# Key-value state in eight full steps of four heads, in a Hedgehog attention with a gated MLP

## The chip, the cores and the metric

The kernel runs on one core of one Trainium2 chip. The metric is the time of one execution on the device in microseconds (us). The engines are named as in the profile: PE is TensorE (matmuls; PEld its weight loads), DVE is VectorE, ACT is ScalarE, POOL is GpSimd, and SP issues most of the DMAs.

## The reference

One sequence of S = 2048 tokens with D = 640 features, 32 heads of 20 features, an MLP of F = 1536:

```python
xn = layernorm(x)
q, k, v = split_heads(xn @ wqkv)                       # 32 heads of 20
phi_q = concat([softmax(q @ w_phi), softmax(-q @ w_phi)])   # 40 features a head
phi_k = concat([softmax(k @ w_phi), softmax(-k @ w_phi)])
kv  = sum_s phi_k[s].T @ v[s]                          # 40 x 20 for each head
z   = sum_s phi_k[s]                                   # 40 for each head
o   = (phi_q @ kv) / (phi_q @ z + 1e-6)
s   = merge_heads(o) @ wo
g   = silu(gelu(xn @ w1 + b1) @ w2 + b2)
out = x + s * g
```

All is float32. The large products are computed in three passes of split operands (high x high, high x low, low x high; `PASSES`), each at fp32r.

## The kernel before

**The first part, up to about 249 us in the profile,** walks over 16 tiles of 128 tokens. For each tile t the keys are projected (`project`, L331), turned into features (`feat1`, `feat2`, `key_fin`: maxima, exponentials, sums for each head), and the values are projected into a tile `v` whose 32 heads stand 21 columns apart: 20 values and a column of ones, which makes the normaliser z with the same matmul. After every second tile, `kv_pair` calls `kv_acc` for the last two finished tiles, so there are eight such calls.

**`kv_acc`** adds one tile of tokens to the key-value state, in one PSUM bank `kv`. Every head h is one matmul in full float32 (L402): its 32 columns of `v` are the weights (20 values, the ones, and columns that belong to the next head and are ignored), its 40 columns of features are streamed. The output has 32 partitions, so four heads fit side by side, on partitions 32e to 32e + 31 with e = 0 to 3. A step is one value of s: the heads that write columns 40s to 40s + 39. Heads stand in groups of three, because a block of 120 feature rows (three heads) is what the later steps use; there are eleven such groups, the last with two heads. Group 4g + e stands on the partitions of e, in columns 120g to 120g + 119. So g = 0 and 1 give three steps each of four heads, and g = 2 gives two steps of three heads and one of two: nine steps.

**The state afterwards.** `kv_rest` (L600) adds the last pair and copies the bank into the tile `kvr` (three activations; the parts without a head are set to zero by two memsets of POOL). `kv_norm` (L623), in the first unit of the MLP, brings the row of z of each e to DRAM in the order of the heads (four stores, one more for the last group), and loads it back broadcast to all partitions (`zrep`, `zf`). `kv_state` (L610), in unit 6 of the MLP, transposes `kvr` in three matmuls, and builds from it the block-diagonal weights: `bdk`, ten blocks of 120 rows and 64 columns, each three heads (L616, one masked copy on DVE), and `bdl` for the last two heads (L620, three copies). `num` (L780, L787) multiplies them by the features of the queries, in the last part.

**The second part, from about 249 to 546 us,** is the MLP, in 12 units (two halves of the tokens by six groups of 256 hidden features). A unit has 54 matmuls of the first layer (`part`, L649) and 60 of the second (`down`, L678), 512 columns each. Beside them the queries of the tiles are normalised by z (`q_norm`, L724 the first step of it on POOL) and written transposed to DRAM (`phi_t`). The eight PSUM banks go round: `bankB()` takes the next one, and a bank comes back after eight allocations.

**The third part** is the output projection (`finish`, L833) for four chunks of 512 tokens, the gate and the residual.

The order of instructions is written out by hand: `phase1` for PE and SP, `startup` and `ffn` for all engines. SP issues its DMAs strictly in the order of the code.

**Buffers.** On-chip memory is given out in the order of the pools: `const` (with `bdk`, `bdl`, and at its end `kvr`), then `slabs` (23 buffers of 5120 bytes in each partition), `rows` (11 of 2816), `small`, and behind them `xpool` and later `late`. Some tiles only fill space:

```python
    xpool.tile([P, 16], F32, name="xpad")
    const.tile([P, 8], F32, name="align")
```

Of the kernel before, what the change touches and what calls it, by code (L numbers as in the profile page):

```python
# [8 lines left out]
F32 = mybir.dt.float32  # L9
F32R = mybir.dt.float32r  # L10
AF = mybir.ActivationFunctionType
OP = mybir.AluOpType
AX = mybir.AxisListType

S, D, H, DH, F = 2048, 640, 32, 20, 1536
P = 128
NT = S // P
# [8 lines left out]
NFT = 11  # L26
# [20 lines left out]
def hedgehog_gated_mlp_kernel(ctx: ExitStack, tc: tile.TileContext, x, xt_in, wqk, bd, wv, wo, w1, b1, w2, b2, out_t):  # L47
    nc = tc.nc
    const = ctx.enter_context(tc.tile_pool(name="const", bufs=1))
# [31 lines left out]
    def slab(dt, name, shape=(P, 2, D)):  # L81
        return slabs.tile(list(shape), dt, tag="S", name=name)
# [7 lines left out]
    def bankB(name="pB"):  # L90
        return pools["B"].tile([P, 512], F32, tag="B", name=name)
# [7 lines left out]
    z_dram = dram.tile([1440], F32, name="z_dram")  # L99
    st_dram = dram.tile([NT // 2, 2, P, 2], F32, name="st_dram")  # L100

    ident = const.tile([P, P], F32, name="ident")
# [13 lines left out]
    mask = const.tile([P, 3], F32, name="mask")  # L116
# [17 lines left out]
    bdk = const.tile([P, 10, 64], F32, name="bdk")  # L134
# [251 lines left out]
    kvp = [None]  # L386
# [6 lines left out]

    def kv_acc(t, phi, v):
        ps = kvp[0]
        for g in range(3):
            for r in range(3):
                for e in range(4):
                    h = 3 * (4 * g + e) + r
                    if 4 * g + e < NFT and h < H:  # L400
                        s = 3 * g + r
                        nc.tensor.matmul(ps[32 * e:32 * e + 32, 40 * s:40 * s + 40], v[:, 21 * h:21 * h + 32],  # L402
                                         phi[:, 40 * h:40 * h + 40], start=t == 0 and s == 0, stop=t == NT - 1,
                                         skip_group_check=True)

    vs, es, phis, xns, wk_s, wq_s = {}, {}, {}, {}, [], []

    def kv_pair(t):
        for u in (t, t + 1):
            kv_acc(u, phis.pop(u), vs.pop(u))  # L410
# [55 lines left out]
    one = nc.const_aps.tensor(1.0, [P, P], F32)  # L466
# [126 lines left out]
    t = NT - 1  # L593
# [5 lines left out]

    def kv_rest():  # L600
        kv_pair(NT - 2)
        kvr = const.tile([P, 360], F32, name="kvr")
        nc.gpsimd.memset(kvr[64:96, 320:360], 0.0)
        nc.gpsimd.memset(kvr[96:, 240:360], 0.0)
        for p, a, b in ((P, 0, 240), (96, 240, 320), (64, 320, 360)):
            nc.scalar.activation(kvr[:p, a:b], kvp[0][:p, a:b], AF.Copy)
        return kvr


    def kv_state(kvr):  # L610
        nc.gpsimd.memset(bdk[:, :, 60:], 0.0)
        ps = bankB()
        for g, m in enumerate((P, P, 96)):
            nc.tensor.transpose(ps[:120, g * P:g * P + m], kvr[:m, 120 * g:120 * g + 120], ident[:m, :m])
        s3 = ps[:120, :320].rearrange("p (f r) -> p f r", r=32)
        nc.vector.tensor_tensor(bdk[:120, :, :60].rearrange("p f (h d) -> p f h d", d=20),  # L616
                                s3[:, :, None, :20].to_broadcast([120, 10, 3, 20]),
                                mask[:120, None, :, None].to_broadcast([120, 10, 3, 20]), op=OP.mult)
        for r in range(3):
            nc.vector.tensor_tensor(bdl[:80, 40 * r:40 * r + 40].rearrange("p (h d) -> p h d", d=20),  # L620
                                    ps[:80, None, 320:340].to_broadcast([80, 2, 20]),
                                    mask[:80, :2, None].to_broadcast([80, 2, 20]), op=OP.mult)
    def kv_norm(kvr):  # L623
        zv = z_dram.rearrange("(g e r) -> e g r", e=4, r=120)
        for e, m in enumerate((3, 3, 2, 2)):
            nc.sync.dma_start(zv[e:e + 1, :m], kvr[32 * e + 20:32 * e + 21, :120 * m].rearrange("p (g r) -> p g r", r=120))
        nc.sync.dma_start(z_dram[1200:2 * D].unsqueeze(0), kvr[84:85, 240:320])
        zf = slab(F32, "zrep")[:].rearrange("p a b -> p (a b)")
        nc.sync.dma_start(zf, z_dram[:2 * D].partition_broadcast(P))
        return zf  # L630
# [132 lines left out]
    def load_phi(c, js, home=None):  # L763
        out = {}
        for j in js:
            ph = slab(F32, "phT", (P, 2, CW)) if home is None else home.tile([P, 2, CW], F32, tag="L", name="phT")
            if j < 5:
                nc.sync.dma_start(ph[:120], phi_t[c][240 * j:240 * j + 240, :].rearrange("(e p) t -> p e t", p=120))
            else:
                nc.sync.dma_start(ph[:80, 0], phi_t[c][1200:, :])  # L770
            out[j] = ph
        return out
# [78 lines left out]
    def w2_raw(g):  # L851
        return [load_raw(w2[f * P:(f + 1) * P, :]) for f in range(g * GF, (g + 1) * GF)]

    kvr = kv_rest()
    e_last = feat1(project(next(queries), wq_s))
    startup.close()
# [6 lines left out]
    for unit in range(units):  # L863
        h, g = divmod(unit, NG)
# [13 lines left out]
        else:  # L878
            wo_r = [load_raw(wo[j * P:(j + 1) * P, :]) for j in range(5)]
            phi = load_phi(ORDER[0], range(6))  # L880
# [52 lines left out]
        if unit == 0:  # L933
            zf = kv_norm(kvr)
# [29 lines left out]
        if unit == NG:  # L964
            kv_state(kvr)
# [123 lines left out]
```

## Time and profile before

| | us |
|---|---|
| median of 3 runs | 662.39 |
| lowest, highest | 662.28, 663.07 |
| the profiled execution | 662.16 |
| its span, first to last instruction | 660.5 |

| engine | busy us | share of the span | instructions |
|---|---|---|---|
| PE | 655.2 | 99% | 4447 |
| DVE | 473.0 | 72% | 720 |
| POOL | 381.2 | 58% | 351 |
| ACT | 228.2 | 35% | 321 |

The granted clock of TensorE was 1.000 over the span. The DMAs moved 126.05 MB, 191 GB/s on average. In the rows that follow, a row of the chain has its start and its length in us, the engine, the tile and the line, and xN instructions. A row of an engine's timeline has start, length, engine, line, operation, tiles, shape and count, and in brackets the idle time before it and what ended that.

### The profile page before, as it was taken

The numbers are of one execution on the slowest core, as the hardware profiler recorded it, in microseconds if no ns is written. First come the engines' busy times: TensorE is split into PE (matmuls) and PEld (weight loads), VectorE is DVE, ScalarE is ACT, GpSimd is POOL, SyncE is SP. The second block draws the span as 40 slices with busy tenths as digits, with TensorE's granted clock in tenths as the row PEclk, the third lists the DMA queues.
The fourth block names the chain that finished last, engine by engine and source line by source line (L and its number), as shares of the span: only waits on it lengthen the run. The fifth ranks groups of instructions, "written<-read, shape, count | busy, mean of one in ns | idle before, by whom it ended". The sixth has DMA issues, their size and how long they took to land.

```text
span 660.5 us, 11388 instructions
## 1 busy us (share of the span) xinstructions
PE 655.2 (99%) x4447; PEld 568.5 (86%) x4447; DVE 473.0 (72%) x720; ACT 228.2 (35%) x321; POOL 381.2 (58%) x351
## 2 busy tenths in 40 slices
PE   9999999999999999999999999999999999999997
PEld 8999999999999998888888888888888886776776
DVE  5887665888777556768978968759889899753232
ACT  3523213332332227352452454751232425113220
POOL 3654254849477456857778776364472966343231
PEclk9999999999999999999999999999999999999999
DMA  8920142834272226537899799695769499999942
GB/s 322 340 81 1 6 152 87 250 82 156 42 200 77 95 88 224 175 107 251 235 249 313 182 414 331 95 338 217 157 219 236 93 273 210 311 232 265 282 169 80
DMA packets 157950, 126.05 MB, mean 191 GB/s; under 512 B 88656, under 2 KB 125520, under 8 KB 157000
## 3 DMA queue, kind: packets, MB, share of 16 engines
q1 hardware_dynamic: 155592, 114.84, 60.3%
q10 hardware_dynamic: 2304, 10.49, 4.3%
q8 instruction: 35, 0.57, 0.3%
q14 instruction: 19, 0.16, 0.1%
HBM read 80.20 MB, written 45.10 MB: 190 GB/s over the span
## 4 chain that ended last, share of the span: by engine, by line
PE 93%; DMA 4%; DVE 1%; POOL 1%; issue 0%; SPq 0%; ACT 0%; POOLq 0%
PE pA L331 28%; PE pB L678 25%; PE pB L649 22%; PE pB L833 11%; PE pB L780 3%; PE kv L402 2%; DMA xt<-in_x_dram 2%; DMA raw<-in_wv_dram 1%; DMA folds<-in_wqk_dram 1%; PE pA L172 1%; PE pB L787 1%; POOL wv L147 0%; DMA st_dram<-pst 0%; PE pA L317 0%; POOL e L352 0%
## 5 line engine op out<-in xcount | busy, mean ns | idle before, releaser
L678 PE MATMUL pB<-hs,w2s 128*128 128x512 f32 x720 | 166.0, 390 | 0.0
L678 PEld LDWEIGHTS pB<-hs,w2s 128*128 128x128 f32 x720 | 134.9, 188 | 29.5 <-DVE oT L784 0.8
L649 PE MATMUL pB<-xp,w1s 128*128 128x512 f32 x324 | 81.3, 389 | 0.0
L649 PE MATMUL pB<-xd,w1s 128*128 128x512 f32 x324 | 79.3, 389 | 0.0
L833 PE MATMUL pB<-oT,wo 128*128 128x512 f32 (+2 forms) x315 | 73.3, 384 | 0.0
L357 ACT ACTIVATE e<-e 128x1280 f32<-128x1280 f32 x32 | 40.7, 1273 | 91.9 <-POOL e L352 91.4
L649 PEld LDWEIGHTS pB<-xd,w1s 128*128 128x128 f32 x324 | 60.8, 188 | 12.6
L649 PEld LDWEIGHTS pB<-xp,w1s 128*128 128x128 f32 x324 | 60.8, 188 | 12.6
L833 PEld LDWEIGHTS pB<-oT,wo 128*128 128x128 f32 x315 | 57.6, 188 | 16.0 <-DVE oT L784 1.6
L370 POOL TENSOR_TENSOR eq<-eq,rc 128x1280 f32<-128x1280 f32 x16 | 37.9, 2368 | 55.9 <-DVE rc L737 38.7
L370 POOL TENSOR_TENSOR e<-e,rc 128x1280 f32<-128x1280 f32 x16 | 39.0, 2439 | 47.4 <-DVE rc L390 47.1
L687 DVE TENSOR_TENSOR y<-pB,y 128x512 f32<-128x512 f32 x100 | 63.1, 676 | 1.4 <-PE pB L678 1.4
L352 POOL TENSOR_TENSOR e<-nr,e 128x640 f32<-128x640 f32 x32 | 45.6, 1425 | 29.9 <-DVE nr L351 26.6
L331 PE MATMUL pA<-wv,xp 128*128 128x320 f32 x384 | 60.5, 310 | 0.3 <-POOL wv L147 0.3
L331 PE MATMUL pA<-wk,xp 128*128 128x320 f32 x384 | 59.7, 310 | 0.0
L654 ACT ACTIVATE pB<-pB,b1t 128x512 f32<-128x512 f32 x48 | 31.8, 662 | 78.8 <-DVE pB L916 28.9
L331 PE MATMUL pA<-wq,xp 128*128 128x320 f32 x384 | 58.8, 309 | 0.1
L331 PEld LDWEIGHTS pA<-wv,xp 128*128 128x128 f32 x384 | 57.0, 188 | 0.5 <-POOL wv L147 0.5
L331 PEld LDWEIGHTS pA<-wq,xp 128*128 128x128 f32 x384 | 56.9, 188 | 0.3 <-PE pA L331 0.3
L331 PEld LDWEIGHTS pA<-wk,xp 128*128 128x128 f32 x384 | 56.9, 188 | 0.1
L724 POOL TENSOR_TENSOR ez<-eq,zrep 128x1280 f32<-128x1280 f32 x16 | 47.3, 2958 | 1.4 <-DMA eq<-e_dram 1.4
L430 POOL TENSOR_TENSOR w1s<-raw,w1s 128x640 fp32r<-128x640 f32 (+1 forms) x18 | 27.0, 1498 | 31.9 <-ACT w1s L429 31.9
(138 smaller groups left out, 996.1 us busy)
## 6 DMA issues: line engine op xcount, KB each, us to landing
raw<-in_w_dram SPq DMA_DIRECT2D x42, 320.0 KB, 4.8
e_dram<-e ACTq DMA_DIRECT2D x16, 640.0 KB, 3.5
eq<-e_dram SPq DMA_DIRECT2D x16, 640.0 KB, 5.7
phi_t<-eq SPq DMA_DIRECT2D x64, 160.0 KB, 3.2
phT<-phi_t SPq DMA_DIRECT2D x20, 480.0 KB, 9.7
xt<-in_x_dram SPq DMA_DIRECT2D x16, 320.0 KB, 7.1
xres<-in_xt_dram SPq DMA_DIRECT2D x20, 256.0 KB, 9.2
out_dram<-xres SPq DMA_DIRECT2D x18, 256.0 KB, 5.8
```

Of the source, the lines that this page charges most:

```text
L331: nc.tensor.matmul(ps[:, hf, :HALF], stat_x(q, o, k, a), ws[k][:, b, hf * HALF:(hf + 1) * HALF], start=n == 0, stop=n == 3 * KC - 1)
L352: nc.gpsimd.tensor_tensor(e5[:, :, :, 1, :], nr[:, :, :, None].to_broadcast([P, 2, 16, DH]), e5[:, :, :, 0, :], op=OP.subtract)
L357: nc.scalar.activation(ef, ef, AF.Exp)
L370: nc.gpsimd.tensor_tensor(e3, e3, rc[:, :, None].to_broadcast([P, 64, DH]), op=OP.mult)
L430: nc.gpsimd.tensor_tensor(sl[:, 1, :n], src, sl[:, 0, :n].bitcast(F32), op=OP.subtract)
L649: nc.tensor.matmul(bank[ch][:], tl[:, a, off + wo_:off + wo_ + P], mov(blk, b), start=new and n == 0, stop=n == len(mms) - 1, skip_group_c ...
L654: nc.scalar.activation(ps, ps, AF.Gelu_apprx_tanh, bias=b1t[:, f:f + 1])
L678: nc.tensor.matmul(ps[:], ws[i][:, b, d * P:(d + 1) * P], hs[o][i][:, a, :], start=i == n == 0, stop=(i, n) == (GF - 1, 2), skip_group_che ...
L687: nc.vector.tensor_tensor(y, ps[:], y, op=OP.add)
L724: nc.gpsimd.tensor_tensor(zv, ef, zf, op=OP.mult)
L780: nc.tensor.matmul(po[64 * e:64 * e + 64, :], bdk[:120, 2 * j + e, :], ph[:120, e, :], start=True, stop=True)
L833: nc.tensor.matmul(ps[:, mv], w, o[:, mv], start=n == 0, stop=n == 15, skip_group_check=True)
```

## The change

`kv_acc` gets eight steps of four heads. The first six are as before (groups 0 to 7). The last eight heads, 24 to 31, are spread over the four positions: heads 24 + 2e and 25 + 2e stand on the partitions of e, in columns 240 to 319. The groups of three that the later steps want are put together in `kv_state`: `kvr` has 400 columns, the last 80 a second copy of columns 240 to 319, so that windows of 120 columns can be transposed (four transposes of 128 rows), and DVE takes each head from the block where it lies (five masked copies for `bdk`, three for `bdl`). `kv_norm` stores two pieces for every e, eight stores in all. The two memsets go, since no part of the bank is empty.

```diff
     def kv_acc(t, phi, v):
         ps = kvp[0]
-        for g in range(3):
-            for r in range(3):
-                for e in range(4):
-                    h = 3 * (4 * g + e) + r
-                    if 4 * g + e < NFT and h < H:
-                        s = 3 * g + r
-                        nc.tensor.matmul(ps[32 * e:32 * e + 32, 40 * s:40 * s + 40], v[:, 21 * h:21 * h + 32],
-                                         phi[:, 40 * h:40 * h + 40], start=t == 0 and s == 0, stop=t == NT - 1,
-                                         skip_group_check=True)
+        for s in range(8):
+            for e in range(4):
+                h = 3 * (4 * (s // 3) + e) + s % 3 if s < 6 else 24 + 2 * e + s - 6
+                nc.tensor.matmul(ps[32 * e:32 * e + 32, 40 * s:40 * s + 40], v[:, 21 * h:21 * h + 32],
+                                 phi[:, 40 * h:40 * h + 40], start=t == 0 and s == 0, stop=t == NT - 1,
+                                 skip_group_check=True)
...
     def kv_rest():
         kv_pair(NT - 2)
-        kvr = const.tile([P, 360], F32, name="kvr")
-        nc.gpsimd.memset(kvr[64:96, 320:360], 0.0)
-        nc.gpsimd.memset(kvr[96:, 240:360], 0.0)
-        for p, a, b in ((P, 0, 240), (96, 240, 320), (64, 320, 360)):
-            nc.scalar.activation(kvr[:p, a:b], kvp[0][:p, a:b], AF.Copy)
+        kvr = const.tile([P, 400], F32, name="kvr")
+        nc.scalar.activation(kvr[:, :320], kvp[0][:, :320], AF.Copy)
+        nc.scalar.activation(kvr[:, 320:], kvp[0][:, 240:320], AF.Copy)
         return kvr
 
 
     def kv_state(kvr):
         nc.gpsimd.memset(bdk[:, :, 60:], 0.0)
         ps = bankB()
-        for g, m in enumerate((P, P, 96)):
-            nc.tensor.transpose(ps[:120, g * P:g * P + m], kvr[:m, 120 * g:120 * g + 120], ident[:m, :m])
-        s3 = ps[:120, :320].rearrange("p (f r) -> p f r", r=32)
-        nc.vector.tensor_tensor(bdk[:120, :, :60].rearrange("p f (h d) -> p f h d", d=20),
-                                s3[:, :, None, :20].to_broadcast([120, 10, 3, 20]),
-                                mask[:120, None, :, None].to_broadcast([120, 10, 3, 20]), op=OP.mult)
+        for i, o in enumerate((0, 120, 240, 280)):
+            nc.tensor.transpose(ps[:120, i * P:(i + 1) * P], kvr[:, o:o + 120], ident[:])
+
+        def heads_of(f, n, blk, h, m):
+            src = ps[:120, 32 * blk:32 * (blk + n)].rearrange("p (f r) -> p f r", r=32)
+            nc.vector.tensor_tensor(bdk[:120, f:f + n, 20 * h:20 * (h + m)].rearrange("p f (h d) -> p f h d", d=20),
+                                    src[:, :, None, :20].to_broadcast([120, n, m, 20]),
+                                    mask[:120, None, h:h + m, None].to_broadcast([120, n, m, 20]), op=OP.mult)
+
+        heads_of(0, 8, 0, 0, 3)
+        heads_of(8, 1, 8, 0, 2)
+        heads_of(8, 1, 9, 2, 1)
+        heads_of(9, 1, 13, 0, 1)
+        heads_of(9, 1, 14, 1, 2)
         for r in range(3):
             nc.vector.tensor_tensor(bdl[:80, 40 * r:40 * r + 40].rearrange("p (h d) -> p h d", d=20),
-                                    ps[:80, None, 320:340].to_broadcast([80, 2, 20]),
+                                    ps[:80, None, 352:372].to_broadcast([80, 2, 20]),
                                     mask[:80, :2, None].to_broadcast([80, 2, 20]), op=OP.mult)
+
     def kv_norm(kvr):
-        zv = z_dram.rearrange("(g e r) -> e g r", e=4, r=120)
-        for e, m in enumerate((3, 3, 2, 2)):
-            nc.sync.dma_start(zv[e:e + 1, :m], kvr[32 * e + 20:32 * e + 21, :120 * m].rearrange("p (g r) -> p g r", r=120))
-        nc.sync.dma_start(z_dram[1200:2 * D].unsqueeze(0), kvr[84:85, 240:320])
+        zv = z_dram[:960].rearrange("(g e r) -> e g r", e=4, r=120)
+        zl = z_dram[960:2 * D].rearrange("(e r) -> e r", e=4)
+        for e in range(4):
+            one = kvr[32 * e + 20:32 * e + 21]
+            nc.sync.dma_start(zv[e:e + 1], one[:, :240].rearrange("p (g r) -> p g r", r=120))
+            nc.sync.dma_start(zl[e:e + 1], one[:, 240:320])
         zf = slab(F32, "zrep")[:].rearrange("p a b -> p (a b)")
```

## The prediction

> **What bounds the kernel now.** I read the first page first, for the engine that carries the span and for the chain that ended last.
>
> ```profile
> PE 655.2 (99%) x4447; PEld 568.5 (86%) x4447; DVE 473.0 (72%) x720; ACT 228.2 (35%) x321; POOL 381.2 (58%) x351
> PE 93%; DMA 4%; DVE 1%; POOL 1%; issue 0%; SPq 0%; ACT 0%; POOLq 0%
> PE pA L331 28%; PE pB L678 25%; PE pB L649 22%; PE pB L833 11%; PE pB L780 3%; PE kv L402 2%; DMA xt<-in_x_dram 2%; DMA raw<-in_wv_dram 1%; DMA folds<-in_wqk_dram 1%; PE pA L172 1%; PE pB L787 1%; POOL wv L147 0%; DMA st_dram<-pst 0%; PE pA L317 0%; POOL e L352 0%
> ```
>
> TensorE (PE) is busy for 99% of the span and is 93% of the chain. Next I asked for what TensorE ever waited, and then for the chain in order of time.
>
> ```profile
> PE pA L469 <- PEq L1079: 0.8, 1, 0.8
> PE pA L172 <- DMA folds<-in_wqk_dram: 0.6, 1, 0.6
> PE pA L331 <- POOL wv L147: 0.3, 1, 0.3
> ```
>
> ```profile
> 2.19 4.89 DMA xt<-in_x_dram
> 7.09 7.19 DMA raw<-in_wv_dram
> 14.29 6.81 DMA folds<-in_wqk_dram
> ...
> 27.68 3.49 PE pA L331 x22
> ...
> 47.21 1.42 PE kv L402 x119
> ...
> 243.12 1.42 PE kv L402 x119
> ...
> 261.40 13.60 PE pB L678 x60
> ...
> 421.88 0.30 PE pB L614 x3
> ```
>
> The waits answer has only these three rows for TensorE, 1.7 us in all. Two lie in the start-up, the third ends at 27.68 us. From there to 657 us no row names another engine or a transfer that TensorE waited for, so a nanosecond saved there shortens the run, and one added lengthens it, until some other engine becomes late. The key-value accumulation, L402, stands on that chain as eight bursts of 1.42 us, one for each pair of token tiles (the first at 47.21, the last at 243.12). The wide matmuls around it (L331, L678, L649, L833) are 86% of the chain.
>
> **Part 1, the accumulation: eight steps instead of nine.** No instruction is removed: a token tile still has 32 matmuls, one for each head, and the order of all engines outside the lines of the diff is unchanged in the compiled program. What changes is how they stand in the four column positions of the array. Before, a tile has six steps of four heads, two of three and one of two; after, eight of four. Whether that saves time depends on what a step costs. The answer for line L402 and the number of its records begun by a given moment of the first burst show it (columns: stretch, its length, busy time of PE and records in it, clock, DMA share, GB/s):
>
> ```profile
> L402 PEld LDWEIGHTS kv<-e,v x1024: 105/112/118, 47.1 to 244.3; 128*32 128x32 f32 x171
> L402 PE MATMUL kv<-e,v x1024: 202/202/224, 47.1 to 244.3; 128*32 128x40 f32 x171
> ...
> 47.10:47.38 0.28, 0.23 (x24) 1.00 0.00 0
> 47.10:47.45 0.35, 0.30 (x32) 1.00 0.00 0
> ...
> 47.10:47.59 0.49, 0.45 (x48) 1.00 0.00 0
> 47.10:47.66 0.56, 0.52 (x54) 1.00 0.00 0
> 47.10:47.73 0.64, 0.59 (x60) 1.00 0.00 0
> 47.10:47.77 0.67, 0.63 (x64) 1.00 0.00 0
> 47.10:48.43 1.33, 1.28 (x128) 1.00 0.00 0
> ```
>
> 1024 records for 512 matmuls: each is two records, so a full step is eight. From 24 to 48 records, three full steps, take 0.22 us: some 72 ns each. The next two stretches add six records each, a step of three heads, and take 0.07 us: as long as a full one. Only the step of two heads is shorter here (four records in some 36 ns). So a step is paid by its position, not by its heads. I read it as two passes of 36 ns in each of the columns. Eighteen steps then give 18 x 72 = 1.30 us for a burst; the last window has 1.28.
>
> The saving for a burst, by that reading: the last record starts, from the first, after 17 x 72 + 36 + 7 = 1267 ns now (the last step has two heads, and neighbours start 7 ns apart), and after 15 x 72 + 36 + 21 = 1137 ns in the new order. That is 130 ns, and for eight bursts 1.04 us. From below: if the two-head step really costs 36 ns, the first tile's 64 records (0.63 us) become 0.576 us, 55 ns for a tile and 0.88 us for 16. From above: two eighteenths of 1.42 us, 0.158 us, times eight: 1.26 us. I take 1.04, the value that also explains the whole burst, with the ends 0.88 and 1.26.
>
> The Trainium skill has a rule that speaks against this: TensorEngine Tiling, section Instruction Overhead, gives every matmul a fixed cost of about 60 cycles, however short it is. If the instruction and not the step paid that, 128 records would cost the same in any order, and the sum would be without this term. The rows above disagree, since six records take the time of eight.
>
> What is late next if this time goes? Most of 1.04 us comes out before 250 us, in steps of 0.13 us, and the vector engines there wait for TensorE and shift with it. I book no loss.
>
> **Part 2, the state.** The final read of the sums becomes two activations instead of three, two memsets of POOL go. Neither is on the chain; booked at nothing. In `kv_state` TensorE has four transposes of 128 rows instead of 128, 128 and 96. The chain gives 0.30 us for three, so 0.10 for one more and up to 0.03 for the wider one: +0.13 us, fully on the chain. DVE has five masked copies in place of one:
>
> ```profile
> 424.59 0.77 DVE L616 TENSOR_TENSOR bdk<-pB,mask 120x600 f32<-120x600 f32 x1
> 425.28 0.39 DVE L620 TENSOR_TENSOR bdl<-pB,mask 80x40 f32<-80x40 f32 x3
> 425.78 2.63 DVE L685 COPY y<-pB 128x512 f32<-128x512 f32 x4
> 429.08 0.69 DVE L685 COPY y<-pB 128x512 f32<-128x512 f32 x1 [0.67 <-PE pB L678]
> ...
> L620 DVE TENSOR_TENSOR bdl<-pB,mask x3: 175/175/175, 425.3 to 425.5; 80x40 f32<-80x40 f32 x3
> ```
>
> 600 elements took 0.77 us and 40 took 0.175, so 480 take about 0.64, and four of 20 or 40 at most 0.175 each: 1.34 against 0.77, +0.57 us. Behind them stand the four copies of L685, and then a copy that waited 0.67 us for TensorE. That wait hides 0.57 us, narrowly; without it a copy would be some 0.1 us late, and the bank that `kv_state` fills is taken again only eight allocations later, in the next unit. Zero, with 0.1 as the upper end.
>
> **Part 3, the normaliser's DMAs.** SP issues eight small stores in `kv_norm` instead of five, then the broadcast load.
>
> ```profile
> 250.27 2.76 SPq L626 DMA_DIRECT2D z_dram<-kvr  x4
> 253.07 0.41 SPq L627 DMA_DIRECT2D z_dram<-kvr  x1
> 255.29 0.35 SPq L629 DMA_DIRECT2D zrep<-z_dram  x1
> 255.74 0.53 SPq L718 DMA_DIRECT2D eq<-e_dram  x1
> 256.32 3.09 SPq L153 DMA_DIRECT2D raw<-in_w_dram  x4
> 267.55 0.59 SPq L698 DMA_DIRECT2D xhi<-xp_dram  x1
> ...
> 275.57 2.96 POOL L724 TENSOR_TENSOR ez<-eq,zrep 128x1280 f32<-128x1280 f32 x1
> 278.47 3.11 POOL L147 TENSOR_TENSOR w2s<-raw,w2s 128x640 fp32r<-128x640 f32 x2
> ```
>
> Three more at up to 2.76 / 4 = 0.69 us each: the broadcast, the load of eq and the four weight loads behind it go out up to 2.1 us later. SP is done with them at 259.41 and has nothing to issue until 267.55, 8.1 us later, so the delay ends there. Their first readers on POOL stand at 275.57 and 278.47, some 20 us behind the issue. No cost.
>
> **The sum.** -1.04 + 0.13 = -0.91 us. The profiled execution took 662.16 us (its span is 660.5): 661.25. The median of the three runs is 662.39, 0.23 above it, so for a median 661.48, and I say 661.5. With the ends, -1.26 + 0.10 and -0.88 + 0.23 (the 0.13 and DVE's 0.1), it is 661.2 to 661.7. The three runs spread over 0.79 us (662.28 to 663.07); with half of that on either side the forecast's own range is 660.8 to 662.1.
>
> **What the diff hides: addresses.** `kvr` grows from 360 to 400 columns, 1440 to 1600 bytes in each partition. It is the last tile of the first pool, so every slab, row, small tile and the x buffers behind it move up by 160 bytes. In the compiled programs the first slab starts at byte 6912 (27 x 256) before and at 7072 after; slabs have a pitch of 5120 and rows of 2816 bytes, multiples of 256, so nearly all big operands now start 160 past a 256-byte line, and 32 past a 64-byte line. No row of this trace has a wide operand placed so. That makes the rivals.
>
> **Rival 1, slower: wide matmuls read shifted operands more slowly.** Place: the four wide lines, 86% of 660.5 us, 568 us. Price: 5.7 us for each per cent; at 1% the time is 661.5 + 5.7 = 667.2. It turns the sign from 0.91 us, 0.16%, and passes the bound below from some 2.2 us, 0.4%: 0.9 ns on a matmul of 13.60 / 60 = 0.227 us. Against it: the accumulation already reads keys at steps of 160 bytes, so every second head starts 32 past a 64-byte line, and its records last 202 ns in minimum and median; weights at steps of 84 bytes load in 105 to 118; the three DVE writes of L620, 160 bytes apart, last 175 each. For it: all these are short, and a start-up cost could hide in them. 0.22, with 664 to 667 us.
>
> **Rival 2: transfers to shifted buffers cost more in the start-up.** Until 27.68 us the chain has three transfers, 4.89 + 7.19 + 6.81 = 18.89 us, and the DMA engines are full:
>
> ```profile
> 0.70:27.68 26.98, 25.93 (x182) 25.21 (x182) 18.11 (x34) 13.01 (x18) 14.04 (x38) 1.00 0.98 360
> ```
>
> Share 0.98. A row of 640 values is 2560 bytes: ten blocks of 256 on a line, eleven when shifted. At worst 10% of 18.89, +1.9 us: 663.4; at half of it 662.4. Against it: the fold weights already lie in DRAM at a row pitch of 3200 bytes, every second row off the line, inside this window at 360 GB/s. 0.15. The rule is that of the Trainium skill, DMA: Bandwidth & Descriptors, section How a descriptor splits into AXI transactions: a transaction must start on a 256-byte address, and the bytes in front of an unaligned start still cost beats. It says this of reading and not of the SBUF writes that count here; no run here shows those yet.
>
> **Rival 3: the change does not do what it says.** If the records and not the steps are paid, the bursts stay 1.42 us, and only the transposes remain: 662.39 + 0.13 = 662.5. The six-record stretches speak against it; for it, the four-record step that took 36 ns. 0.08.
>
> **How the numbers follow.** Forecast 0.55, rivals 0.22, 0.15 and 0.08. About 0.2%, 1.3 us, is what a measurement of this kernel can tell from no change, so faster is below 661.07 and slower above 663.71. The forecast centres 0.4 us above the first of these, and its range reaches 0.3 below it: 0.22 of its 0.55 counts as faster. Rival 1 is slower, with 0.04 of rival 2 where both add up: 0.26. The rest is within the bound: 0.52. The range starts at 660.8 and goes to 665.0, into rival 1, with about 0.15 above and 0.04 below left out.
>
> **What would show each step.** Right: eight bursts of L402 in the chain at about 1.29 us instead of 1.42; 64 records begun 0.58 us into a burst; four transposes at about 0.43 us; the wide lines at the same mean durations and pitch, 13.60 us for 60 of L678; the start-up ending near 27.7 us. Wrong: bursts still at 1.42 (rival 3); L331 starting its unbroken run at 28.5 us or later (rival 2); 60 matmuls of L678 over 13.65 us (rival 1); new rows of TensorE waiting for DVE near 429 us or for the raw weights near 275 us.

## The result, and the profile after

| | before | after |
|---|---|---|
| median, us | 662.52 (6 runs, 662.28 to 663.87) | 667.66 (6 runs, 665.33 to 668.96) |
| ratio, 95% interval | | 1.0072 [1.006, 1.0083] |
| the profiled execution, its span, us | 662.16, 660.5 | 668.96, 667.2 |

The change made the kernel slower by 4 to 5.5 us. The profiled execution is the slowest of the six, 1.3 us above their median. The page of the changed kernel, busy time, packets and chain (behind the edits the lines have moved down by 6: L684 is the old L678, L655 L649, L839 L833, L786 L780):

```profile
PE 658.4 (99%) x4448; PEld 568.2 (85%) x4448; DVE 472.3 (71%) x724; ACT 228.1 (34%) x320; POOL 380.3 (57%) x349
DMA packets 157952, 126.05 MB, mean 189 GB/s; under 512 B 88658, under 2 KB 125522, under 8 KB 157002
PE 86%; DMA 8%; DVE 2%; POOL 1%; issue 1%; SPq 1%; ACT 0%; POOLq 0%; DVEq 0%; ACTq 0%
PE pA L331 30%; PE pB L684 23%; PE pB L655 22%; PE pB L839 6%; DMA phT<-phi_t 3%; PE kv L399 2%; PE pB L786 2%; PE pA L172 1%; DMA out_dram<-xres 1%; DMA xd_dram<-xhi 1%; DMA folds<-in_wqk_dram 1%; DMA gt<-g_dram 1%; POOL wv L147 1%; DVE oT L790 0%; PE pA L317 0%
```

TensorE's share of the chain fell from 93% to 86%, and the DMAs' rose from 4% to 8%. Four transfers are new on it: `phT<-phi_t`, with which the last part loads the query features, `out_dram<-xres` and `gt<-g_dram` between two of those loads, and `xd_dram<-xhi` in the MLP. What TensorE waited for, and rows of the chain:

```profile
PE pB L786 <- DMA phT<-phi_t: 3.4, 5, 1.1
PE pA L172 <- DMA folds<-in_wqk_dram: 0.9, 1, 0.9
PE pA L466 <- PEq L1085: 0.8, 1, 0.8
PE pA L331 <- POOL wv L147: 0.3, 1, 0.3
```

```profile
28.65 3.49 PE pA L331 x22
...
48.18 1.32 PE kv L399 x124
...
243.34 1.30 PE kv L399 x126
...
261.69 13.60 PE pB L684 x60
...
320.69 7.75 DMA xd_dram<-xhi
...
422.74 0.44 PE pB L609 x4
...
575.61 6.98 DMA phT<-phi_t
...
591.71 5.69 DMA phT<-phi_t
...
617.85 10.61 DMA phT<-phi_t
```

The first row of the waits was not there before. The bursts are shorter, and 60 matmuls of the second layer take 13.60 us as before. Following the same instruction of TensorE through both traces (its start in the engine's timeline) gives the place of the loss:

| TensorE starts | before, us | after, later by |
|---|---|---|
| the unbroken run of L331 | 27.68 | 0.97 |
| first matmul of the MLP | 248.97 | 0.11 |
| second layer of its first unit | 261.23 | 0.30 |
| second layer of its fourth unit | 364.59 | 0.87 |
| the first layer after the transposes | 430.24 | 0.97 |
| `num` of the second chunk | 582.95 | 0.97 |
| second group of `finish` there | 599.56 | 2.84 |
| third | 623.69 | 6.80 |
| last matmul | 656.74 | 6.96 |

So 5.8 us of the 6.96 were lost between 583 and 624 us, far from every edited line. SP's part of the timeline just ahead of that, before and then after, shows what came late:

```profile
548.88 7.09 SPq L746 DMA_DIRECT2D phi_t<-eq  x8
556.07 1.91 SPq L768 DMA_DIRECT2D phT<-phi_t  x3
```

```profile
549.85 13.98 SPq L752 DMA_DIRECT2D phi_t<-eq  x8
563.92 1.99 SPq L774 DMA_DIRECT2D phT<-phi_t  x3
```

The same eight stores of query features kept SP for 13.98 us instead of 7.09, and the loads of those features, next in its order, went out 7.9 us later. SP did not catch up: the next two groups of three such loads went out 7.90 and 7.55 us later than before (591.71 against 583.81, 616.58 against 609.03). TensorE then stood still where before it had no gap (its timeline; in brackets the idle time and what ended it):

```profile
624.77 1.08 PE L786 MATMUL pB<-phT,bdk 120*64 120x512 f32 x4 [0.86 <-DMA phT<-phi_t]
626.92 1.48 PE L786 MATMUL pB<-phT,bdk 120*64 120x512 f32 x4 [1.07 <-DMA phT<-phi_t]
628.59 1.98 PE L786 MATMUL pB<-phT,bdk 120*64 120x512 f32 x4 [0.19 <-DMA phT<-phi_t]
```

The row of waits counts 3.4 us of the 5.8. The last two of these groups of four matmuls take 1.48 and 1.98 us instead of 1.08, and the granted clock was lower there (columns: stretch, its length, busy time of TensorE and its records, clock, DMA share, GB/s):

```profile
626.00:628.00 2.00, 1.08 (x4) 0.87 0.98 304
628.00:630.00 2.00, 1.81 (x6) 0.50 1.03 350
630.00:632.00 2.00, 2.00 (x8) 0.78 1.05 250
```

The missing parts of these three stretches add up to 1.7 us at full clock, an estimate of what the lower clock cost; the rest of the 5.8 was not placed. Only the profiles of e5 and e12 among the experiments below have such a stretch between 28 and 656 us, worth 1.7 us in each. It stands right behind waits for phT in all three, but e2 and e6, with 3.8 us of such waits, have none, so what sets it off is open.

The store is this line of `q_norm`, untouched by the diff; `ef` is the tile `eq`, a slab:

```python
        for a in range(4):
            nc.sync.dma_start(dst[a], ef[32 * a:32 * a + 32, :].rearrange("p (b i) -> p b i", i=32))
```

It cuts each of 32 rows into 40 pieces of 32 floats, 128 bytes. The 64 stores make 64 x 1280 = 81,920 of the 88,658 packets under 512 bytes. Before, a slab starts on a 256-byte line and no piece crosses one. In the changed kernel `eq` starts 160 past a line, its pieces start at 160 and 32, and every second piece crosses a line's end (160 + 128 = 288).

### The profile page after: what moved, and what is told of

It reads as the page before. It is cut to its first block, busy times and chain, and to the rows that moved or that the text cites. A ratio compares the mean times of both kernels' runs of the same rounds, so it can differ in the third digit from the quotient of the medians.

```text
span 667.2 us, 11394 instructions
## 1 busy us (share of the span) xinstructions
PE 658.4 (99%) x4448; PEld 568.2 (85%) x4448; DVE 472.3 (71%) x724; ACT 228.1 (34%) x320; POOL 380.3 (57%) x349
## 2 busy tenths in 40 slices
DMA packets 157952, 126.05 MB, mean 189 GB/s; under 512 B 88658, under 2 KB 125522, under 8 KB 157002
## 4 chain that ended last, share of the span: by engine, by line
PE 86%; DMA 8%; DVE 2%; POOL 1%; issue 1%; SPq 1%; ACT 0%; POOLq 0%; DVEq 0%; ACTq 0%
PE pA L331 30%; PE pB L684 23%; PE pB L655 22%; PE pB L839 6%; DMA phT<-phi_t 3%; PE kv L399 2%; PE pB L786 2%; PE pA L172 1%; DMA out_dram<-xres 1%; DMA xd_dram<-xhi 1%; DMA folds<-in_wqk_dram 1%; DMA gt<-g_dram 1%; POOL wv L147 1%; DVE oT L790 0%; PE pA L317 0%
## 5 line engine op out<-in xcount | busy, mean ns | idle before, releaser
L684 PE MATMUL pB<-hs,w2s 128*128 128x512 f32 x720 | 166.0, 390 | 0.0
L684 PEld LDWEIGHTS pB<-hs,w2s 128*128 128x128 f32 x720 | 134.9, 188 | 29.5 <-DVE oT L790 0.8
L655 PE MATMUL pB<-xp,w1s 128*128 128x512 f32 x324 | 81.7, 390 | 0.1
L655 PE MATMUL pB<-xd,w1s 128*128 128x512 f32 x324 | 79.3, 389 | 0.0
L839 PE MATMUL pB<-oT,wo 128*128 128x512 f32 (+2 forms) x315 | 73.5, 385 | 0.0
L839 PEld LDWEIGHTS pB<-oT,wo 128*128 128x128 f32 x315 | 57.8, 189 | 16.9 <-issue 3.2
L655 PEld LDWEIGHTS pB<-xp,w1s 128*128 128x128 f32 x324 | 60.5, 188 | 13.6 <-ACT x L671 0.7
L655 PEld LDWEIGHTS pB<-xd,w1s 128*128 128x128 f32 x324 | 60.8, 188 | 12.6
L352 POOL TENSOR_TENSOR e<-nr,e 128x640 f32<-128x640 f32 x32 | 43.9, 1373 | 30.0 <-DVE nr L351 27.6
L331 PE MATMUL pA<-wv,xp 128*128 128x320 f32 x384 | 60.5, 310 | 0.3 <-POOL wv L147 0.3
L331 PE MATMUL pA<-wk,xp 128*128 128x320 f32 x384 | 59.7, 310 | 0.0
L331 PE MATMUL pA<-wq,xp 128*128 128x320 f32 x384 | 58.8, 309 | 0.0
L331 PEld LDWEIGHTS pA<-wv,xp 128*128 128x128 f32 x384 | 57.0, 188 | 0.5 <-POOL wv L147 0.5
L331 PEld LDWEIGHTS pA<-wq,xp 128*128 128x128 f32 x384 | 56.9, 188 | 0.2 <-issue 0.2
L331 PEld LDWEIGHTS pA<-wk,xp 128*128 128x128 f32 x384 | 56.9, 188 | 0.1
```

What stands on the lines that cost most here:

```text
L331: nc.tensor.matmul(ps[:, hf, :HALF], stat_x(q, o, k, a), ws[k][:, b, hf * HALF:(hf + 1) * HALF], start=n == 0, stop=n == 3 * KC - 1)
L352: nc.gpsimd.tensor_tensor(e5[:, :, :, 1, :], nr[:, :, :, None].to_broadcast([P, 2, 16, DH]), e5[:, :, :, 0, :], op=OP.subtract)
L655: nc.tensor.matmul(bank[ch][:], tl[:, a, off + wo_:off + wo_ + P], mov(blk, b), start=new and n == 0, stop=n == len(mms) - 1, skip_group_c ...
L684: nc.tensor.matmul(ps[:], ws[i][:, b, d * P:(d + 1) * P], hs[o][i][:, a, :], start=i == n == 0, stop=(i, n) == (GF - 1, 2), skip_group_che ...
L839: nc.tensor.matmul(ps[:, mv], w, o[:, mv], start=n == 0, stop=n == 15, skip_group_check=True)
```

## The experiments

All ratios are to the kernel before, timed beside it on the same chip. "Slabs" and "rest" say how far past a 256-byte line the slabs, and the rows, small tiles and x and late buffers behind them, start. "Crossing" is the share of the features' pieces that cross a line's end. The last two columns are SP's row for the eight stores near 550 us and TensorE's waits for phT, of the profiled execution.

| run | slabs, rest | crossing | us | ratio, 95% interval | eight stores, us | waits for phT, us |
|---|---|---|---|---|---|---|
| the changed kernel | 160, 160 | half | 667.66 | 1.0072 [1.006, 1.0083] | 13.98 | 3.4 |
| e1_after_on256 | 0, 0 | none | 662.39 | 0.9999 [0.999, 1.0009] | 9.79 | none |
| e2_before_160 | 160, 160 | half | 668.32 | 1.0088 [1.0071, 1.0105] | 13.38 | 3.8 |
| e3_before_128 | 128, 128 | none | 663.20 | 1.0011 [0.9997, 1.0024] | 8.11 | 0.2 |
| e4_before_8stores | 0, 0 | none | 662.40 | 0.9997 [0.9987, 1.0006] | 7.34 | none |
| e5_before_64 | 64, 64 | half | 667.17 | 1.0069 [1.0054, 1.0084] | 13.46 | 3.0 |
| e6_before_32 | 32, 32 | half | 667.56 | 1.0078 [1.0063, 1.0093] | 13.61 | 3.8 |
| e7_slabs_160 | 160, 0 | half | 671.05 | 1.0131 [1.0094, 1.0168] | 11.04 | 1.4 |
| e8_rest_160 | 0, 160 | none | 668.65 | 1.0093 [1.0078, 1.0108] | 7.50 | none |
| e9_piece_192 | 0, 0 | all | 676.27 | 1.0196 [1.0171, 1.022] | 15.11 | 5.5 |
| e10_piece_0 | 0, 0 | none | 662.76 | 1.0002 [0.9992, 1.0012] | 8.27 | 0.4 |
| e11_slabs_64 | 64, 0 | half | 670.80 | 1.0113 [1.008, 1.0146] | 12.89 | 4.3 |
| e12_rest_64 | 0, 64 | none | 665.88 | 1.0055 [1.0037, 1.0072] | 9.48 | 2.9 |
| e13_after_piece_0 | 160, 160 | none | 664.01 | 1.0018 [1.0003, 1.0033] | 9.66 | 0.2 |
| e14_piece_64 | 0, 0 | none | 662.48 | 0.9998 [0.9989, 1.0007] | 8.77 | none |
| e15_after_on256_ms | 0, 0 | none | 661.97 | 0.9993 [0.9984, 1.0001] | 9.52 | none |

**Addresses or edits?** The first run (e1) is the changed kernel with 96 bytes more in a filler tile, which brings the slabs back to a line (7168 = 28 x 256). The second (e2) is the kernel before with a filler of 160 bytes behind `kvr`, and none of the change. The third (e3) has 128 bytes there. The fourth (e4) has only the stores of z cut into eight.

```diff
# e1, of the changed kernel
-    const.tile([P, 8], F32, name="align")
+    const.tile([P, 32], F32, name="align")
# e2, of the kernel before, behind kvr (e3: 32 columns, e5: 16, e6: 8)
+        const.tile([P, 40], F32, name="kpad")
# e4, of the kernel before
-        for e, m in enumerate((3, 3, 2, 2)):
-            nc.sync.dma_start(zv[e:e + 1, :m], ...)
+        for e, g0, g1 in ((0, 0, 2), (0, 2, 3), (1, 0, 2), (1, 2, 3), (2, 0, 1), (2, 1, 2), (3, 0, 2)):
+            nc.sync.dma_start(zv[e:e + 1, g0:g1], ...)
```

> The changed kernel with 96 bytes more of filling, so that the first slab starts at byte 7168, a multiple of 256, and every buffer behind it is on the 256-byte lines again; all instructions and their order are those of the changed kernel. If the shifted addresses cost the time: start-up ends near 27.7 us, the last part waits for no phT, bursts of 1.32 us stay, four transposes stay at 0.44: 662.5 - 8 x 0.10 + 0.13 = about 661.8 us. If the three added stores or the new state do: about 667.7 us, as the changed kernel.

> The kernel before, with 160 unused bytes behind kvr and nothing else: every slab, row and x buffer starts 160 past a 256-byte line, as in the changed kernel. If the addresses cost the time: 667.7 + 0.7 (the bursts keep 1.42 us, three transposes) = about 668.4 us, start-up ending near 28.6 us, TensorE waiting for phT in the last part. If the stores or the state do: 662.5 us.

> The kernel before with 128 unused bytes behind kvr: all big buffers start 128 past a 256-byte line, still on a 64- and a 128-byte line. If a transfer pays for every 256-byte line that it crosses: slower, start-up ending after 28 us, 665 to 669 us. If only the place against 64 or 128 bytes counts: 662.5 us.

> The kernel before with the normaliser's five small stores cut into eight pieces of the same bytes; addresses as before. If the three more DMAs ahead of the broadcast load cost the time (each later transfer then waits for another one of its predecessors): about 667 us. If the addresses do: 662.5 us, the broadcast load up to 2 us later with nobody waiting.

The edits without the shift cost nothing (662.39 against 662.70 of the kernel before beside it), the shift without the edits costs all of it, and the eight stores of z cost nothing. The shifted kernel before shows nearly the rows of the changed one, in SP's timeline and in TensorE's waits:

```profile
550.12 13.38 SPq L747 DMA_DIRECT2D phi_t<-eq  x8
```

```profile
PE pB L781 <- DMA phT<-phi_t: 3.8, 4, 1.3
```

It is not the wide matmuls: with both operands shifted alike, their means are within 1 ns of the kernel before (390 ns for L678, 389 for both groups of L649). The groups by line of e2:

```profile
L679 PE MATMUL pB<-hs,w2s 128*128 128x512 f32 x720 | 166.0, 390 | 0.0
L650 PE MATMUL pB<-xp,w1s 128*128 128x512 f32 x324 | 81.5, 390 | 0.1
L650 PE MATMUL pB<-xd,w1s 128*128 128x512 f32 x324 | 79.3, 389 | 0.0
```

A shift of 128 bytes, which puts no piece across a line's end, costs at most 0.24%.

**Which shifts, and which buffers?** Two smaller shifts of everything, then the slabs and the rest apart, with a filler pool between them:

```diff
# e7, slabs alone at 160 (e11, at 64: 48 and 16 columns)
+    gap = ctx.enter_context(tc.tile_pool(name="gap", bufs=1))
+    gap.tile([P, 24], F32, name="gpad")
...
+        const.tile([P, 40], F32, name="kpad")
# e8, the rest alone at 160 (e12, at 64: 16 columns)
+    gap = ctx.enter_context(tc.tile_pool(name="gap", bufs=1))
+    gap.tile([P, 40], F32, name="gpad")
```

> The kernel before with 64 unused bytes behind kvr: all big buffers 64 past a 256-byte line, off the 128-byte lines, on the 64-byte ones. If the loss at 160 comes from leaving the 64-byte lines: like 128 past, 662.5 to 663.2 us. If it comes from the 128-byte lines: about 668 us.

> The kernel before with 32 unused bytes behind kvr: all big buffers 32 past a 256-byte line, off the 64-byte lines as at 160. If the 64-byte line decides: about 668 us, with TensorE waiting for phT in the last part. If it is a property of 160 past a 256-byte line (a first piece of 96 bytes): 662.5 to 664 us.

> The kernel before with only the slabs moved by 160 bytes (160 unused bytes ahead of them, 96 behind, so rows, small tiles, x buffers and the late pool are on 256-byte lines). The slabs hold eq, which the phi_t stores read in pieces of 128 bytes, half of the phT buffers, the query features and the MLP's hidden values. If the slow phi_t stores make the last part late: 666 to 668 us, with a start-up ending as before near 27.7. If the loads into rows and x buffers do: 662.5 us.

> The kernel before with everything behind the slabs moved by 160 bytes (rows, small tiles, x buffers with the fold weights, late pool), the slabs on their lines. If the phi_t stores make the loss: 662.5 to 663.5 us, with up to 1 us lost in the start-up, whose rows and fold weights are moved. If the loads into rows and the late pool do: 666 to 668 us.

Shifts of 64 and 32 are as slow as 160, and 128 is not: the time goes with whether half of the pieces cross, and not with the size of the shift. Slabs and rest apart were meant to share out the loss, and brought one of their own: with weights (in slabs) and moving operand (x) at different places, every matmul of L649 takes longer, 395 to 396 ns:

```profile
L652 PE MATMUL pB<-xp,w1s 128*128 128x512 f32 x324 | 83.7, 396 | 0.1
L652 PE MATMUL pB<-xd,w1s 128*128 128x512 f32 x324 | 81.5, 395 | 0.0
```

(slabs alone, e7). Each of the 12 units then loses 0.4 us. The profiled execution of e8 is 4.75 us behind at the end of the MLP and 5.8 at its last matmul, with the stores at 7.50 us and no wait for phT. That says less than was asked: slower units also give the transfers more time, so a transfer that is late at full pace may not be late here. That is argued and was not tried.

**The stores by themselves.** These three leave every address of the kernel before as it was, and only read all 40 pieces of a row from one place:

```diff
# e9: 48:80, byte 192; e10: 0:32, byte 0; e14: 16:48, byte 64
-            nc.sync.dma_start(dst[a], ef[32 * a:32 * a + 32, :].rearrange("p (b i) -> p b i", i=32))
+            src = ef[32 * a:32 * a + 32, 48:80]
+            nc.sync.dma_start(dst[a], src[:, None, :].to_broadcast([32, 40, 32]))
```

> The kernel before with every address as it was; only the source of the stores of the query features (phi_t) is changed: each of the 40 pieces of 128 bytes that a row is cut into is read from one and the same place of the features, byte 192 past a 256-byte line, so that each piece crosses that line. This kernel leaves out the other 39 pieces: the query features in DRAM, and so the output, are not the reference's. Theory of the stores (pieces that cross a line are read slowly, the features come to DRAM late, the last part waits for them): the last eight stores, 7.09 us of SP's time before, take over 11 us, TensorE waits 3 to 5 us for phT, and the time is 665.5 to 669. Rival (what counts is where the loads of the last part land, or the wide operands, which are on the line here): eight stores at 7 to 8 us, time 662.4 +- 0.7.

> As the run with pieces at byte 192, but each of the 40 pieces is read at byte 0 of a 256-byte line, so that none crosses anything; the other 39 pieces are left out in the same way. Theory of the stores: the last eight take about 7 us, as before (there too no piece crosses a line), and the time is 662.4 +- 0.7. Rival (reading one place 40 times is slow by itself, whatever its address): slow as the run at byte 192, in which case that run shows nothing.

> The kernel before, its addresses as they were; each of the 40 pieces is read at byte 64 of a 256-byte line: it crosses the middle of the line (byte 128) and not its end. The other 39 pieces are left out. If only the end of a 256-byte line counts: as with pieces at byte 0, eight stores at 7 to 8.3 us, time 662.7 +- 0.7. If 128 bytes count too: eight stores near 15 us, time 673 to 677.

That shows the mechanism. The three differ only in the byte at which a piece is read. Across the end of a 256-byte line it costs 13.7 us; on the line, or across the line's middle, nothing. SP's timeline and TensorE's waits of e9, SP's of e10, and SP's of e14:

```profile
556.89 15.11 SPq L747 DMA_DIRECT2D phi_t<-eq  x8
572.10 2.10 SPq L769 DMA_DIRECT2D phT<-phi_t  x3
```

```profile
PE pB L781 <- DMA phT<-phi_t: 5.5, 6, 1.1
PE pB L649 <- ACT x L665: 3.2, 2, 1.8
PE pB L649 <- DVE pB L917: 2.9, 3, 1.5
```

```profile
549.43 8.27 SPq L747 DMA_DIRECT2D phi_t<-eq  x8
557.79 1.87 SPq L769 DMA_DIRECT2D phT<-phi_t  x3
```

```profile
548.79 8.77 SPq L747 DMA_DIRECT2D phi_t<-eq  x8
557.66 1.86 SPq L769 DMA_DIRECT2D phT<-phi_t  x3
```

With all pieces crossing, the stores make even the MLP wait: TensorE was 7.86 us late at the end of it. In the changed kernel, the 0.57 us lost between 327 and 365 us lie where e9 lost its first 3.85 us of the MLP, and are gone in the profiled execution of the next run, e13.

**How much of the changed kernel's loss is that?** The changed kernel with all its addresses, its pieces read from a place on the line (byte 96 of `eq`), and the two runs of slabs or rest at 64:

```diff
# e13, e16, e17, of the changed kernel
-            nc.sync.dma_start(dst[a], ef[32 * a:32 * a + 32, :].rearrange("p (b i) -> p b i", i=32))
+            src = ef[32 * a:32 * a + 32, 24:56]
+            nc.sync.dma_start(dst[a], src[:, None, :].to_broadcast([32, 40, 32]))
```

> The changed kernel with all its addresses; only the source of the stores of the query features is changed: each of the 40 pieces of a row is read from one and the same place that lies on a 256-byte line (byte 96 of the features, which start 160 past a line). The other 39 pieces are left out, so the query features and the output are not the reference's. Theory (the stores carry the whole loss): eight stores near 549 us take 7 to 8.3 us instead of 13.98, TensorE waits under 0.6 us for phT, time 662.5 to 663.5 (0.97 us are behind at 583 us in the changed kernel's profile, and what lies off the line besides stays). Rival (landing the loads in shifted buffers has its own share, as the run with the rest at 64 suggests): eight stores at 7 to 8.3 us, but 1 to 3 us of waits for phT, time 664 to 666.

> The kernel before; the 23 slabs start 64 past a 256-byte line, everything behind them starts on the line. Theory of the stores: the features lie in a slab, so the last eight stores take about 13 us and the time is 667 (666 to 668.5); by 64 the wide matmuls keep their 389 ns, if what slowed them in the run with slabs alone at 160 was the place of the two operands against each other in 64 bytes. Rival 1 (the place in 256 bytes counts for the matmuls): L649 at 395 ns, as with 160, and the time 670 or more. Rival 2 (what lies behind the slabs is what counts): 662.4.

> The kernel before; the slabs on the line, everything behind them 64 past one. Theory of the stores: the features stay on the line, eight stores at about 7 us, time 662.4 (661.9 to 663.2), L649 at 389 ns. Rival 1 (the place in 256 bytes counts for the matmuls): L649 at 395 ns and 667. Rival 2 (what lies behind the slabs counts): 666 to 668.

> The changed kernel with its store pieces on the line once more (39 of 40 pieces left out, as there), for a profile of another execution. If what remains lies in transfers: an execution over 663.5 us shows waits of TensorE for phT of 1 us or more after 583 us, or a start-up that ends later than 28.2 us, and the wide matmuls keep 389 and 390 ns. If it lies in the matmuls: their means rise.

> A second execution of the same kernel, with the same two expectations: waits for phT of 1 us or more or a start-up past 28.2 us in an execution over 663.5 us, against wide matmuls with higher means.

667.66 becomes 664.01: 3.65 of the 5.14 us are the stores', some 70%. About 1.5 us stay (0.2 to 2.2 by the interval), so that the stores' share lies between a little over half and nearly all of the loss, and the ten executions of e13 spread from 661.57 to 667.07. The profiled one, at 661.89, had nothing to place. Two further profiled executions (e16, e17) took 664.42 and 663.80 us, and TensorE's waits in them name the place:

```profile
PE pB L787 <- DMA phT<-phi_t: 2.1, 3, 1.1
```

```profile
PE pB L787 <- DMA phT<-phi_t: 1.8, 2, 1.1
```

The start-up ended at 27.84 and 27.81 us, the wide matmuls kept 389 and 390 ns, and the stores took 8.89 and 8.63 us. Up to 583 us both executions were ahead of the kernel before, by 0.36 and 0.53 us. So in these two the rest of the loss lies in the last part's transfers too, with the pieces on the line. It does not come from the eight stores near 550 us: the loads behind them left SP 1.4 and 1.0 us later than before, less than the 2.75 us of e1, in which TensorE waited for none. By 613 us they left 4.6 and 4.2 us later, so SP fell behind after those stores. The run with the rest at 64 points the same way: 2.9 us of waits for phT with the slabs on the line (its profiled execution took 670.51 us, far above its median, 1.7 us of which is the lower clock). Which of the transfers of that part carries it (phT, gates, residual, output) was not tried.

The slabs at 64 were expected at 389 ns for L649, if 64 bytes were the unit that counts; they took 394 (and the rest at 64: 392 and 391). That guess fell.

**Where the saved time went.** The changed kernel on the line, with the two memsets of POOL back on an unused tile:

```diff
# e15, of e1
-    const.tile([P, 32], F32, name="align")
+    msp = const.tile([P, 32], F32, name="align")
...
+        nc.gpsimd.memset(msp[64:96, :], 0.0)
+        nc.gpsimd.memset(msp[96:, :], 0.0)
```

> The changed kernel with its slabs on the line, and two memsets of POOL on an unused tile where the removed ones stood. If the 0.18 us that unit 0 of the MLP lost hangs on POOL being earlier there: unit 0 takes 12.27 us again, and the time is 0.2 below the run with the slabs on the line, about 662.2, ratio 0.9993. If not: unit 0 at 12.45 and 662.4, ratio 0.9999.

The first unit of the MLP took its old time again (12.27 us; 12.26 before, 12.45 in e1). But this profiled execution came into the unit 0.18 us later than e1, so in both the unit ended at the same moment, 0.07 us earlier than in the kernel before. 661.97 against 662.55 is 0.9993, with an interval that just holds 1. No version here is shown to beat the kernel before.

## Why the prediction was wrong, point by point

**The step that failed** is "What the diff hides: addresses". It saw that `kvr` moves everything by 160 bytes and put the right rule beside it, but asked only what this does to reads by matmuls (rival 1) and to loads into shifted buffers in the start-up (rival 2). It did not go through the transfers that read from the shifted buffers, of which the 64 stores in pieces of 128 bytes are by count more than half of all packets. The sum booked addresses at nothing, the range ended at 665.0, and 667.66 lies above it. The chain of the kernel before has no phT row, so the stores had slack there. That slack was used up by 6.9 us more on one group of eight, and reading the pieces on the line gave back 3.65 of the 5.14 us (e13). Which transfer carries the rest of the loss is open.

**The rule.** The prediction cited the Trainium skill, DMA: Bandwidth & Descriptors, section How a descriptor splits into AXI transactions, for writes, and said itself that the section speaks of reading. For the reads of these stores it does speak: a piece at byte 192 needs two transactions, one at byte 0 or 64 needs one. The runs agree with that count (676.27 against 662.76 and 662.48). They do not tell it from the section's count of beats, which is, as an estimate from its rules, ten for the piece at 192, six for the one at 64 and four for the one at 0.

**Rival 1** came out at a time near the right one for a wrong reason: 667.2 was its price for 1%, but L678 x60 stayed at 13.60 us. Slower matmuls were seen only where the two operands are shifted against each other (e7, e8, e11, e12), which the change doesn't do.

**Rival 2** would have shown in L331 starting at 28.5 us or later, and it did start at 28.65. But this start moves from execution to execution: 28.14 with everything shifted (e2), 28.11 at 128, 28.16 on the line (e15), 27.93, 27.84 and 27.81 in three profiles of the changed kernel's addresses. So the 0.97 us of the profiled execution can't be put down to the addresses; most of it is likely chance. The mark was badly chosen: one profile of before gave no spread. What the rival says of loads into shifted buffers may be the 1.5 us left over, at the other end of the run.

**Rival 3** fell, the bursts are shorter. **Part 1** was right in kind and mis-sized: 0.10 us a burst (0.12 the last), 0.82 in all, against 1.04 and below the lower end of 0.88. The windows of the first burst, from 0.11 us ahead of it as before (busy time and records of TensorE, then of its weight loads), and the rows of the line:

```profile
L399 PEld LDWEIGHTS kv<-e,v x1024: 105/111/118, 48.1 to 244.4; 128*32 128x32 f32 x171
L399 PE MATMUL kv<-e,v x1024: 201/202/224, 48.1 to 244.4; 128*32 128x40 f32 x171
...
48.07:48.70 0.63, 0.59 (x63) 0.59 (x66) 1.00 0.00 0
48.07:48.72 0.65, 0.61 (x66) 0.61 (x70) 1.00 0.00 0
...
48.07:49.32 1.25, 1.21 (x128) 1.21 (x128) 1.00 0.05 13
```

The first tile's 64 records take 0.60 us, where 0.58 was forecast and 0.63 stood before: a full step costs 75 ns rather than 72, as the x48 row of the prediction (0.45 us for six steps) already had it. The three steps that were not full then cost 0.63 - 6 x 0.075 = 0.18 us together, less than three full ones (0.225), so that less is saved when they go: 0.03 us in this tile, against the 0.055 of the lower end. All 128 records have begun by 1.25 us instead of 1.33, which is near the 0.10 of the chain.

**Part 2** held. The transposes took 0.44 us, 0.14 more (0.13 forecast). DVE's five masked copies took 1.02 us for 0.77, less than the 1.34 booked, and the copy behind them still waited for TensorE, 0.60 instead of 0.67 us:

```profile
425.46 1.02 DVE L613 TENSOR_TENSOR bdk<-pB,mask 120x480 f32<-120x480 f32 x5
426.41 0.39 DVE L623 TENSOR_TENSOR bdl<-pB,mask 80x40 f32<-80x40 f32 x3
427.73 3.08 DVE L691 COPY y<-pB 128x512 f32<-128x512 f32 x5 [0.94 <-DVE bdl L623]
431.41 0.69 DVE L691 COPY y<-pB 128x512 f32<-128x512 f32 x1 [0.60 <-PE pB L684]
```

**Part 3** held. The weight loads behind the stores of z went out 1.15 us later (257.47 against 256.32; up to 2.1 booked), no wait of TensorE near 275 us followed, and e4 is at 0.9997.

**"I book no loss"** for the time saved in the bursts was too plain. With the addresses right (e1), 0.82 us of bursts left 0.26 at the start of the MLP: the start-up took 0.14, a wait for DVE 0.4. That wait stands in e10 as well (0.3), whose first part is that of before, so it is no price of the change. The prediction read the chain from 27.68 us on as TensorE's alone, because TensorE never waited there. But the chain of the kernel before leaves TensorE at 73 us and comes back only at 89.62, by a load of x and then VectorE:

```profile
79.92 5.96 DMA xt<-in_x_dram
...
89.39 0.20 DVE nr L351
...
89.62 9.04 PE pA L331 x60
```

TensorE started there 0.04 us after VectorE was done, so there was no slack. In e1 the same load took 6.13 us, and a store ahead of it 3.03 instead of 2.83; VectorE was done 0.3 us later, and TensorE waited. Time saved on TensorE ahead of that point reaches the end only if these transfers are no slower. The first unit took 0.19 back and the transposes 0.13. The whole change without its shift was forecast at -0.91 us; measured were -0.31 (e1; -0.66 to +0.6 by its interval) and -0.58 (e15; -1.06 to +0.07). The forecast lies outside the first interval and inside the second, whose kernel has the two memsets back: a gain is not shown, and one as large as forecast is unlikely.

## What to carry to other kernels

A tile that grows in the first pool moves all that lies behind it: write out the new start of every buffer, and go through every transfer that reads from it or writes to it, those cut into small pieces first. An added 96 bytes of filler was worth more here than the edit could gain. Before a mark in the start-up is taken as proof of anything, look at how far it moves between profiles of kernels that are alike there.

## What the runs showed of the hardware that was not expected

- Stores that read 128-byte pieces on chip are slow when a piece crosses the end of a 256-byte line, and of the places tried only then: eight stores kept SP for 7.09 to 9.79 us where none crosses, and for 11.04 to 15.11 where half or all do. Crossing byte 128 of a line costs nothing (662.48 us).
- In three profiles the granted clock of TensorE fell to 0.50 for some two us right behind waits for loads, and cost about 1.7 us each time (an estimate, from stretches such as 0.87, 0.50 and 0.78 over two us each). Two profiles with waits as long kept 1.00.
- A matmul of 128 x 512 whose weights and moving operand start at different places of a 256-byte line lasts longer: 389 and 390 ns with both on the line or both 160 past it, 391 to 394 with one of them 64 past, 395 and 396 with one 160 past. What in the array or its reads makes this is open.
